# A spectral mixer with an MLP on one core: another element order in the array behind the first transform's last stage, and four placed pieces moved by one or two steps

## The chip, the cores and the metric

The kernel runs on one core of a Trainium2 chip. The metric is the device time of one execution in microseconds (us). Five engines work side by side, each through its own queue in order: PE (matrix multiplication; it first loads a stationary operand, the weights, and then streams the moving one), ACT and DVE (elementwise work, and copies out of PE's result memory PSUM into the working memory SBUF, called evictions here), POOL and SP (in this kernel almost only queues that start DMA transfers). An engine that waits for another holds up everything behind it in its own queue.

## The reference: what is computed

```
X = np.fft.rfft(x, axis=1)                      # x: 8 batches x 3008 rows x 256 channels
Y = X * (filt_r + 1j * filt_i)                  # one complex factor per frequency and channel
y = np.fft.irfft(Y, n=3008, axis=1)             # back to 24064 rows x 256
h = y @ w_in                                    # 256 -> 2048
g = np.maximum(h, 0.0) + alpha * np.minimum(h, 0.0)
out = g @ w_out                                 # 2048 -> 256
```

Inputs and output are fp32; the kernel works in fp16 with fp32 sums in PSUM.

## The kernel before, in words

3008 = 94 x 32, so each transform is two short ones with a factor between them. Both are matrix multiplications with constant tables. A batch goes through stages a (94-point, forward), b (32-point with factors, and the filter multiplied in on DVE), c (32-point back) and d (94-point back). Between a and b, and between c and d, rows and columns must change places.

**Batches one to seven** (class Fft) change them by writing to DRAM and reading back. Their pieces are placed among the steps of the MLP. The MLP runs over 48 blocks of 512 rows (the sixth of every twelve has 384); each block has 16 steps; a step is `up(j)` (two matmuls of w_in, L481; at odd j the eviction L490 on ACT, then L493 and L495 on DVE) and `down(j)` of the block before (matmuls of w_out, L512, with the eviction L517). `put(step, fn, ...)` writes a list by hand: a piece stands ahead of `up` in its step, and in the steps of the set `front` (those with a piece_a or a piece_c of batches one to seven) `down` stands ahead of both. Nothing reorders this later: the place in the program is the place in each engine's queue.

**Batch zero** (class First) has nothing to hide behind. It runs ahead of the blocks and changes rows and columns on PE, by a multiplication with the unit matrix `id16`:

- `piece_a` (L280) evicts into `am`, which lies in the array gtb, in runs of four results that stand 32 elements apart.
- `turn_at` (L290) turns `am` into `at`, evicted by ACT.
- The loop over kp = 0 to 11 (from L409) issues piece_b of kp + 2 (L299 on PE into one of two hps buffers, then the multiplication L304 on DVE that makes uu), then piece_c of kp (L324, 16 matmuls of 64 columns). Two kp share a pair of psO banks, `ops[0]` and `ops[1]`; the pool psO has just two, so piece_c of the next pair waits for the evictions of this one.
- After every odd kp up to 9, `keep_c` (L333) copies both banks on ACT into the array v (seen flat as `vm`), 512 results in each copy. kp 10 and 11 have copies of their own with 256 results; the second copy of kp 11 is on DVE. All these copies have the line of their helper: L255 on ACT, L258 on DVE.
- After kp 1, 3 and 5 comes a turn_at for later kp. After kp 7, 8 and 9, and within kp 11, stand two matmuls each (`warm`, L376) whose result nobody reads.
- After kp 5, a memset on DVE (L420) is followed on POOL's queue by the loads of w_in, w_out and batch one's x (L422, L424, L112). Behind them come the copies that make `filts_s`, wanted by batch one's piece_b and by the sign changes `neg` (L558) from step 26 on.
- `half_t` and `piece_t` then call `turn` (L340): for one of the 32 time positions s and one half f of the channels, 96 columns of v are the weights (L346) and `id16` streams. Four half_t come ahead of the blocks, the rest (piece_t) in steps 0, 3, 19, 23, 32 and 34.
- `half_d` and `pair_d` (L232) are stage d: eight matmuls for a pair_d into the one buffer of the pool psF, then an eviction into yT, the MLP's input. piece_b of batch one uses psF too (from step 36, every six steps), and DVE frees it at the end of L187.

In both versions a result of keep_c has four indices besides its partition (a channel): g (16: half f and group of four positions), e (4: position within the group), q (4) and k (24). A row of 96 weights is all (q, k) of one g and e. The array's order is e, g, q, k before, the last index running fastest.

Blocks of 512 rows read yT in order: group three of batch zero (rows 2256 to 3007) is first read in step 64, batch one's first group in step 96.

Of the kernel before, what the change touches and what calls it, by code (L numbers as in the profile page):

```python
# [15 lines left out]
NK = 24  # L16
# [34 lines left out]
def kernel(  # L51
# [211 lines left out]
    class First(Fft):  # L263
# [67 lines left out]
            on_act(o, w.unsqueeze(2).to_broadcast([128, 2 * (kb - ka), 2, 32]))  # L331

        def keep_c(self, kp, evicts, n=2):  # L333
            vm = self.vm.rearrange("p (e g q k) -> p g q k e", q=4, k=NK, e=4)
            for e in range(2):
                k = 2 * kp + e
                evicts[e](vm[:, :, :, k : k + 2 * n - 1 : 2],
                          self.ops[e][:, 0:n].rearrange("p k (g q e) -> p g q k e", q=4, e=4))

        def turn(self, pt, i, n):  # L340
            m = self.vm.rearrange("p (e g m) -> p g m e", m=96, e=4)
            for u in range(n):
                for f in range(2):
                    o = 256 * (u % 2) + 128 * f
                    s = n * i + u
                    nc.tensor.matmul(pt[0:96, u // 2, o : o + 128], m[:, 8 * f + s // 4, :, s % 4], id16,  # L346
                                     start=True, stop=True)
# [175 lines left out]
    def put(step, fn, *args):  # L523
        plan.setdefault(step, []).append((fn, args))

    def plan_fft(b, a_at, ta, quarters, x_at, b_at, add, c_at, d_at):
        f = Fft(b)
        for i in range(8):
            put(a_at[i], f.piece_a, i)
            front.add(a_at[i])  # L530
        for c in range(4):
            put(a_at[2 * c + 1], f.save_a, c)
            if b + 1 < NB:
                put(x_at[c],
                    lambda b=b, c=c: xc.update({(b + 1, c): load_x(b + 1, c)}))
        for q in range(quarters):
            w = NK // quarters
            put(ta, f.turn_a, nc.sync, w * q, w * q + w)
        for q in range(6):
            put(b_at[q], f.piece_b, q, not add)  # L540
            if add:
                put(b_at[q] + add, f.piece_s, q)
        for q in range(6):
            put(c_at[q], f.piece_c, q)
            front.add(c_at[q])
            if q % 2 == 1:
                put(c_at[q] + 1, f.turn_c, q // 2)
        for i in range(8):
            put(d_at[i], f.pair_d, i, on_act)

    for g, ts, ds, te, de in ((1, (0, 3), (6, 12), on_act, both[::-1]), (2, (19, 23), (25, 28), on_dve, (on_dve, on_dve)),
                              (3, (32, 34), (39, 45), on_act, (on_act, on_act))):
        for i in range(2):
            put(ts[i], f0.piece_t, 2 * g + i, te)
            put(ds[i], f0.pair_d, 2 * g + i, de[i])
# [7 lines left out]
    def d_steps(p):  # L563
        return [p + t for t in (91, 93, 104, 108, 116, 120, 140, 152)]

    plan_fft(1, range(12, 28, 2), 28, 4, (34, 42, 54, 66), range(36, 72, 6), 0, range(48, 84, 6),
             (91, 93, 97, 100, 111, 121, 142, 154))
    plan_fft(2, (50, 56, 62, 68, 74, 80, 82, 84), 90, 4, (57, 69, 81, 89),
             (106, 116, 126, 136, 148, 158), 7, (116, 126, 136, 148, 158, 172), d_steps(96))
    for b in range(3, NB):  # L570
        p = 96 * (b - 1)
# [54 lines left out]
```

## Time and profile before

| | |
|---|---|
| three runs | 813.82, 807.13, 810.01 us; median 810.01 |
| the profiled execution | 808.31 us; the span of its trace 806.5 us |
| busy in the span | PE 773.3 us (96%), ACT 606.3 (75%), DVE 596.8 (74%), POOL 142.2 (18%) |
| mean granted clock of PE | 0.977 |
| DMA | 100.64 MB, mean 125 GB/s |

How to read the lines below: in a timeline, start and length come first, then the engine, the line of the kernel, the operation, and output <- input with the shape; "x2" merges neighbours; what stands in brackets is the engine's idle time ahead of the instruction and what ended it. Grouped lines end with total busy time, mean of one in ns, and idle time by what ended it. In the slices of the page each digit is a fortieth of the span (about 20 us), in tenths. A tile's view lists minimum, median and maximum in ns, and who waited for it how long in all and how often.

### The profile page before, as it was taken

Reading aid. Unit: us, or ns where it says so; the run is one execution under the profiler, and the core shown is the slowest. Engines: PE = TensorE matmul, PEld = TensorE weight load, DVE = VectorE, ACT = ScalarE, POOL = GpSimd, SP = SyncE. Lnnn points to the kernel's source line nnn. Section 1 sums busy time; section 2 is a strip of 40 time slices with the busy share of each in tenths; the row PEclk is TensorE's granted clock in tenths of the full one; section 3 lists DMA queues with packets and bytes.
Section 4 is the critical chain, followed back from the end, with each engine's and each line's share of the span. In section 5 each row is a group of like instructions: output and inputs, shape, how many; then the busy total and the mean of one; then the engine's idle time right before and its main releaser. Section 6 shows DMA issues by size and latency. Waiting matters only on the chain.

```text
span 806.5 us, 16086 instructions
## 1 busy us (share of the span) xinstructions
PE 773.3 (96%) x6349; PEld 512.2 (64%) x6349; DVE 596.8 (74%) x1116; ACT 606.3 (75%) x673; POOL 142.2 (18%) x271
## 2 busy tenths in 40 slices
PE   7558999999999999999999999999999999999997
PEld 4334656666666666766666666666666666776665
DVE  4427888578887788687886788778886888766664
ACT  4868778788876887688876887688877777676764
POOL 6320056113200122012200221001110111000000
PEclk9559999999999999999999999999999999999999
DMA  9596469875674555935675464843366232521111
GB/s 184 84 174 149 131 97 208 191 200 139 169 145 131 109 140 125 216 91 129 152 136 139 96 165 106 177 127 97 104 130 161 66 87 72 131 66 33 41 40 52
DMA packets 95083, 100.64 MB, mean 125 GB/s; under 512 B 11280, under 2 KB 82464, under 8 KB 94816
## 3 DMA queue, kind: packets, MB, share of 16 engines
q1 hardware_dynamic: 80368, 70.25, 33.4%
q0 software_dynamic: 14640, 29.38, 21.1%
q8 instruction: 49, 0.80, 0.4%
q14 instruction: 26, 0.21, 0.1%
HBM read 55.28 MB, written 46.66 MB: 126 GB/s over the span
## 4 chain that ended last, share of the span: by engine, by line
PE 88%; ACT 6%; DMA 2%; DVE 2%; issue 1%; POOL 0%; ACTq 0%; DVEq 0%; POOLq 0%
PE hps L481 39%; PE op L512 39%; ACT v L255 3%; PE hps L155 3%; PE psF L232 3%; PE psF L179 2%; ACT gtb L490 1%; PE hps L210 1%; DMA uu<-ww 1%; DMA xs<-in_x_dram 1%; PE op L324 1%; DMA zt<-v_dram 1%; DVE ww L186 1%; DVE uu L187 1%; DVE m L493 1%
## 5 line engine op out<-in xcount | busy, mean ns | idle before, releaser
L490 ACT ACTIVATE gtb<-hps 128x1024 f16<-128x1024 f32 (+1 forms) x384 | 385.6, 1005 | 130.4 <-PE hps L481 129.5
L512 PE MATMUL op<-wout_s,gtb 128*128 128x256 f16 x3008 | 435.8, 273 | 0.1
L481 PE MATMUL hps<-yT,win_s 128*128 128x512 f16 (+1 forms) x1536 | 434.0, 375 | 1.6 <-ACT gtb L490 1.4
L512 PEld LDWEIGHTS <-gtb 128*128 128x128 f16 x3008 | 293.9, 98 | 168.4 <-issue 0.4
L493 DVE TENSOR_SCALAR m<-gtb,alm_s 128x512 f16<-128x512 f16 (+1 forms) x768 | 232.9, 346 | 151.2 <-ACT gtb L490 150.4
L495 DVE TENSOR_TENSOR gtb<-gtb,m 128x2048 f16<-128x2048 f16 (+1 forms) x192 | 231.0, 1203 | 10.4 <-PE hps L481 0.5
L481 PEld LDWEIGHTS <-win_s 128*128 128x128 f16 x1536 | 142.5, 98 | 61.2 <-issue 14.7
L193 POOL DMA_DIRECT2D sw<-ww x144 | 70.9, 500 | 381.6 <-DVE ww L186 378.6
L255 ACT ACTIVATE asb<-hps 96x1024 f16<-96x1024 f32 x56 | 57.1, 1020 | 12.0 <-PE hps L155 11.5
L517 ACT ACTIVATE osb<-op 128x512 f32<-128x512 f32 (+1 forms) x97 | 56.2, 580 | 5.3 <-issue 2.8
L255 ACT ACTIVATE yT<-psF 128x752 f16<-128x752 f32 x59 | 47.1, 798 | 12.8 <-PE psF L232 12.7
L112 POOL DMA_DIRECT2D xs<-in_x_dram x64 | 39.2, 709 | 91.1 <-PE hps L155 79.4
L255 ACT ACTIVATE v<-hps 128x1024 f16<-128x1024 f32 x42 | 43.0, 1024 | 15.4 <-PE hps L210 15.4
L186 DVE TENSOR_TENSOR ww<-psF,filts_s 128x1024 f16<-128x1024 f32 x42 | 51.1, 1217 | 0.0
L187 DVE TENSOR_TENSOR uu<-psF,filt_s 128x1024 f16<-128x1024 f32 x42 | 51.0, 1213 | 0.0
L232 PE MATMUL psF<-wi_s,zt 96*128 96x94 f16 x500 | 31.3, 206 | 3.3 <-DVE uu L187 2.6
L155 PE MATMUL hps<-xs,wf_s 94*96 94x512 f16 x112 | 33.5, 380 | 0.6 <-ACT asb L255 0.6
L232 PEld LDWEIGHTS <-zt 96*128 96x128 f16 x512 | 28.7, 99 | 6.8 <-DVE uu L187 3.2
L255 ACT ACTIVATE v<-op 128x512 f16<-128x512 f32 (+1 forms) x12 | 25.5, 2376 | 6.2 <-PE op L324 6.2
L191 POOL DMA_DIRECT2D uu<-ww x24 | 19.3, 1229 | 40.8 <-DVE uu L187 35.6
L304 DVE TENSOR_TENSOR uu<-hps,filt_s 128x1024 f16<-128x1024 f32 x11 | 13.4, 1222 | 17.0 <-PE hps L299 14.6
L198 DVE TENSOR_TENSOR uu<-uu,sw 128x1024 f16<-128x1024 f16 x36 | 24.6, 684 | 0.1
(67 smaller groups left out, 197.6 us busy)
## 6 DMA issues: line engine op xcount, KB each, us to landing
out_dram<-osb SPq DMA_DIRECT2D x160, 128.0 KB
a_dram<-asb SPq DMA_DIRECT2D x28, 384.0 KB
v_dram<-v SPq DMA_DIRECT2D x84, 128.0 KB
zt<-v_dram SPq DMA_DIRECT2D x28, 384.0 KB
sw<-ww POOLq DMA_DIRECT2D x144, 64.0 KB, 2.4
at<-a_dram SPq DMA_DIRECT2D x20, 384.0 KB
xs<-in_x_dram POOLq DMA_DIRECT2D x32, 192.0 KB, 4.3
xs<-in_x_dram POOLq DMA_DIRECT2D x32, 184.0 KB, 6.0
```

Of the source, the lines that this page charges most:

```text
L155: nc.tensor.matmul(ps[0:96, u], wf1_s, xs[:, o : o + 512], start=True, stop=True)
L186: nc.vector.tensor_mul(ww, px, fs)
L187: nc.vector.tensor_mul(uu, px, f)
L193: nc.gpsimd.dma_start(out=sw[o : o + 32], in_=ww[i : i + 32])
L232: nc.tensor.matmul(ps[:, m], self.zt[:, 8 * g + 4 * mh + m, dh * 128 : dh * 128 + 128], wi3_s, start=True, stop=True)
L255: nc.scalar.activation(o, i, AF.Copy)
L481: nc.tensor.matmul(self.hps[:, j % 2, 0:tn], win_s[:, kt, j * 128 : (j + 1) * 128], yT[:, kt, self.t0 : self.t0 + tn], start=(kt == 0), st ...
L490: nc.scalar.activation(g[:, 2 * i : 2 * i + 2], self.hps[:, :, 0:tn], AF.Copy)
L493: nc.vector.tensor_scalar(m[:, 2 * i + h], g[:, 2 * i + h], 0.0, a, OP.min, OP.mult)
L495: nc.vector.tensor_add(g, g, m)
L512: nc.tensor.matmul(self.op[:, si - s0], self.gts[k][:, 128 * si : 128 * si + 128], wout_s[:, k], start=(si == s0 and k == 0), stop=(si == ...
L517: nc.scalar.activation(osb[:, 0:m], self.op[:, 0:m], AF.Copy)
```

## The change

```diff
         def keep_c(self, kp, evicts, n=2):
-            vm = self.vm.rearrange("p (e g q k) -> p g q k e", q=4, k=NK, e=4)
+            vm = self.vm.rearrange("p (g q k e) -> p g q k e", q=4, k=NK, e=4)
...
         def turn(self, pt, i, n):
-            m = self.vm.rearrange("p (e g m) -> p g m e", m=96, e=4)
+            m = self.vm.rearrange("p (g m e) -> p g m e", m=96, e=4)
...
-                              (3, (32, 34), (39, 45), on_act, (on_act, on_act))):
+                              (3, (32, 34), (41, 47), on_act, (on_act, on_act))):
...
     plan_fft(1, range(12, 28, 2), 28, 4, (34, 42, 54, 66), range(36, 72, 6), 0, range(48, 84, 6),
-             (91, 93, 97, 100, 111, 121, 142, 154))
+             (92, 94, 97, 100, 111, 121, 142, 154))
```

The order in v becomes g, q, k, e: the four e of one (g, q, k) stand side by side (8 bytes of fp16), and the 96 weights of one g and e stand 4 elements apart instead of side by side. Copies and loads have the same number, shape and place in the queues. Two pair_d of batch zero's group three stand two steps later, and batch one's first two one step later; on PE and ACT they pass the matmuls and the evictions of those steps. The queues of DVE, POOL and SP hold the same instructions in the same order.

## The prediction

> **What bounds the kernel now.** I read the slices of the page first, then its chain and its groups. PE is at 9 tenths or more in nearly every slice after 60 us, so that part is worth only what PE itself saves. The slices from 20 to 60 us stand apart: PE at 5, ACT at 7 or 8, the granted clock at 5.
>
> ```profile
> PE   7558999999999999999999999999999999999997
> ACT  4868778788876887688876887688877777676764
> PEclk9559999999999999999999999999999999999999
> PE 88%; ACT 6%; DMA 2%; DVE 2%; issue 1%; POOL 0%; ACTq 0%; DVEq 0%; POOLq 0%
> L255 ACT ACTIVATE v<-op 128x512 f16<-128x512 f32 (+1 forms) x12 | 25.5, 2376 | 6.2 <-PE op L324 6.2
> ```
>
> Half of ACT's 6% of the chain is line 255 writing v: the evictions of the first transform's last stage, 2.4 us for 512 elements. The view of tile v tells who waits for them:
>
> ```profile
> L346 PEld LDWEIGHTS <-v x64: 119/123/203, 57.2 to 94.7; 128*96 128x96 f16 x64
> L255 ACT ACTIVATE v<-op x12: 1316/2407/2712, 20.4 to 53.0; 128x512 f16<-128x512 f32 x10, 128x256 f16<-128x256 f32 x2
>   PE op L324: 16.0, 10
> ```
>
> The timeline of one pair of kp shows the loop that this makes (start, length, then what it waited for):
>
> ```profile
> 26.71 1.04 PE L290 MATMUL psF<-id,gtb 128*128 128x128 f16 x8
> 26.80 4.62 ACT L255 ACTIVATE v<-op 128x512 f16<-128x512 f32 x2 [0.93 <-PE op L324]
> 30.93 1.34 ACT L255 ACTIVATE at<-psF 128x1024 f16<-128x1024 f32 x1
> 31.48 0.21 PE L324 MATMUL op<-twi_s,uu 64*128 64x64 f16 x1 [2.01 <-ACT v L255]
> 31.98 0.64 PE L299 MATMUL hps<-at,gtb 64*64 64x256 f16 x8
> 32.68 1.22 DVE L304 TENSOR_TENSOR uu<-hps,filt_s 128x1024 f16<-128x1024 f32 x1 [3.08 <-PE hps L299]
> 33.20 4.63 ACT L255 ACTIVATE v<-op 128x512 f16<-128x512 f32 x2 [0.93 <-PE op L324]
> ```
>
> A round takes 33.20 - 26.80 = 6.4 us: two evictions (4.62), then the next pair of piece_c, held until both psO banks are empty. DVE waits 3 us a round for the same reason. The eviction is the bound here.
>
> **Part 1: the evictions.** Before, keep_c puts four neighbouring results 1536 elements apart, so every 2-byte result goes to a place of its own; after, four stand side by side (8 bytes), in a row of 96 per (q, k). What such a write costs is in the trace: piece_a's eviction also writes runs of four, 32 elements apart, and reads PSUM with a jump at every element. Its row stands beside dense ones (form by form):
>
> ```profile
> L255 ACT ACTIVATE gtb<-hps 128x768 f16<-128x768 f32 x3 | 2.4, 810 | 6.6 <-PE hps L280 6.6
> L255 ACT ACTIVATE zt<-op 96x512 f16<-96x512 f32 x1 | 0.6, 592 | 2.1 <-PE op L346 2.1
> L255 ACT ACTIVATE zt<-psF 96x1024 f16<-96x1024 f32 x4 | 4.1, 1024 | 0.9 <-PE psF L346 0.9
> ```
>
> Dense costs 592 ns at 512 and 1024 at 1024: 0.84 ns an element and some 160 fixed. At 768 that gives 808, and the scattered reader with runs of four took 810. So runs of four are free, and so is the jumping read; I take 592 ns for 512 (from 2310, half of 4.62) and an estimated 380 for 256. The other end is today's 2310. The Trainium skill (Advanced Engine Details and Errata, SBUF Cachelines) says two or more accesses to a 16-byte line run at full rate and a new line per access is penalised; the trace agrees, 2310 against 592, and by it the sum would be the same.
>
> Now the loop's new length, from where ACT ends its table copy (20.5 us, unchanged) to the first half_t:
>
> ```profile
> 20.42 4.61 ACT L255 ACTIVATE v<-op 128x512 f16<-128x512 f32 x2
> 23.75 1.22 DVE L304 TENSOR_TENSOR uu<-hps,filt_s 128x1024 f16<-128x1024 f32 x1 [2.47 <-DMA filt_s<-in_filt_r_dram]
> 33.85 0.06 DVE L420 MEMSET win_s<- 128x1 uint32 x1
> 34.22 1.09 POOL L422 DMA_DIRECT2D win_s<-in_moe_w_in_dram  x2 [9.59 <-DVE win_s L420]
> 37.06 2.12 POOL L112 DMA_DIRECT2D xs<-in_x_dram  x4
> 55.87 1.30 DVE L258 CAST v<-psF 128x256 f16<-128x256 f32 x1 [8.19 <-ACT v L255]
> 56.69 1.95 POOL L434 DMA_DIRECT2D filts_s<-filt_s  x4 [6.58 <-DMA filt_s<-fst]
> 57.23 1.09 PE L346 MATMUL op<-id,v 128*96 128x128 f16 x8 [1.69 <-DVE v L258]
> 61.91 1.46 PE L481 MATMUL hps<-yT,win_s 128*128 128x512 f16 x6
> 69.53 0.60 PE L155 MATMUL hps<-xs,wf_s 94*96 94x512 f16 x2
> ```
>
> The fifth multiplication (kp 4) waits for its filter until 23.75 whatever ACT does. Eight multiplications follow, 8 x 1.22 = 9.8, so uu of kp 11 can't exist before 33.5, and with the last piece_c and its eviction half_t can't start before about 34.5. That is the floor. Walking the loop: a round is the two evictions (1.18), piece_c, piece_b, piece_c on PE (about 0.55 each at the half clock of these rows: piece_c's rest runs from 31.48 to 31.98, piece_b's 0.64 has its tail in it) and waits of some 0.2, about 3.05 us; two warm matmuls (an estimated 1.0: they stream the 1024 columns that L290's eight do in 1.04) come after each of kp 7, 8 and 9. From 23.75 this gives keep of kp 2/3 at 23.0, 4/5 at 27.4, 6/7 at 30.7, 8/9 at 34.8, kp 11 done at 38.7. With PE's terms halved (full clock) DVE's 2 x 1.22 and ACT's 1.18 and 1.34 (the eviction of at) a round set 2.5 us, and kp 11 is done at 35.8. I take 37.0, between them: 57.23 - 37.0 = **20.2 us less**, ends 17.7 (with another us of waits) and 22.7 (the floor).
>
> What else hangs on this: L420's memset stands behind the multiplication of kp 7, at 28.6 instead of 33.85. So win_s, wout_s, batch one's x and fst's copy on POOL's queue come 5.2 us sooner, not 20. Their cover:
>
> ```profile
> win_s<-in_moe_w_in_dram POOLq DMA_DIRECT2D x2, 512.0 KB, 6.4
> xs<-in_x_dram POOLq DMA_DIRECT2D x4, 192.0 KB, 12.3
> 87.61 0.61 DVE L558 TENSOR_SCALAR filts_s<-filts_s,sgn_s 128x1536 f16<-128x1536 f16 x1
> ```
>
> win_s, issued at 29.0 and landing 6.4 us later, is there at 35.5 to 36; the first block, 4.7 us behind half_t, starts at 41.3. Batch one's first x (37.06 + 12.3 - 5.2 = 44.2) is wanted at 69.53 - 20.6 = 48.9. filts_s, copied from 51.5 instead of 56.69, is wanted by the sign change at 87.6 - 20.6 = 67. All covered, by 5, 5 and a few us; if a cover went, that much of the gain would go. With that DMA traffic nearer to the first blocks I add nothing.
>
> **Part 2: the weight loads.** turn now loads its 96 columns with a step of 4 elements (8 bytes). No load in the trace has a step. Today eight pairs take 0.45 us (94.34 to 94.79; the third row is the next step's first matmul, so a step is 0.87):
>
> ```profile
> 94.34 0.61 PE L346 MATMUL psF<-id,v 128*96 128x128 f16 x8
> 94.79 0.59 PE L481 MATMUL hps<-yT,win_s 128*128 128x512 f16 x2
> 95.66 0.59 PE L481 MATMUL hps<-yT,win_s 128*128 128x512 f16 x2
> ```
>
> That is 56 ns each, 128 columns streaming, with the load hidden below. The row nearest to a stepped access is the old eviction, (2310 - 160) / (592 - 160) = 5 times a dense element; five times at most 56 ns is 280, 0.22 more for each of 64 loads: **+14 us at most**. A gain is excluded, since the load is hidden today. I take 0: the moving operand of L324 also hops between runs, and the trace has no PE read slowed by its pattern. Half of that factor (2.5) would cost 0.084 x 64 = 5.4. The Trainium skill speaks against zero: Vector Engine (DVE) Microarchitecture Reference, Measured stream behaviour on trn2, says a VectorE port keeps its rate only for runs of two adjacent 4-byte words and takes up to 2.5 times when stepping single words; by it, if it holds for PE's port, the sum would be about 5 us higher; no run here shows it yet.
>
> **Part 3: the clock in between.** Stretches of 1 us (last columns: granted clock, DMA share, GB/s; PE's busy time comes first):
>
> ```profile
> 21.00:22.00 1.00, 0.24 (x8) 0.09 (x1) 0.29 (x1) 1.00 (x1) 0.53 (x1) 1.00 1.36 194
> 22.00:23.00 1.00, 0.14 (x1) 0.10 (x1) 0.00 (x0) 1.00 (x2) 0.48 (x1) 0.82 0.98 127
> 60.00:61.00 1.00, 0.95 (x13) 0.65 (x11) 0.69 (x2) 0.74 (x2) 0.00 (x0) 0.90 1.06 184
> ```
>
> The clock fell soon after PE went idle at 21.2 and came back at 60.1, after 3 us of turns. In the new loop PE is busy nearly throughout, so it should come back in the 30s. The turns after the loop, 16 pairs at half clock, would save 16 x 0.05 = 0.8; I count **0.4**.
>
> **Part 4: the moved steps.** Rows of the stalls:
>
> ```profile
> 101.54 0.51 PE L232 MATMUL psF<-wi_s,zt 96*128 96x94 f16 x8 [1.80 <-DVE uu L187]
> 108.56 0.51 PE L232 MATMUL psF<-wi_s,zt 96*128 96x94 f16 x8 [0.84 <-DVE uu L187]
> 156.89 0.51 PE L232 MATMUL psF<-wi_s,zt 96*128 96x94 f16 x8 [0.52 <-DMA zt<-v_dram]
> ```
>
> Group three's pair_d (eight matmuls and one ACT eviction each, no DMA) waits at steps 39 and 45 until VectorE frees the only psF buffer. Two steps are 2 x 0.87 = 1.74 us, so at 41 and 47 the waits are about 0.06 and 0. Late next: piece_b at 42 and 48 wants psF back one step later, while ACT's eviction (an estimated 0.79 for 752 by the slope above, and 0.23 of waits) has 0.87 of cover, so 0.15 each. Gain 2.64 - 0.06 - 0.3 = **2.3**, ends 1.0 (ACT late with its queue) and 2.6. yT of group three is wanted at step 64, far off. On ACT each eviction now stands behind one gtb eviction more; POOL's and SP's queues are unchanged. Batch one's first pair_d goes from 91 to 92: one step of 384 columns (an estimated 0.76) covers the 0.52, gain **0.5**. The next from 93 to 94: its yT is wanted at step 96, 1.5 us of steps against 1.05; nothing, or up to -0.5 if ACT is late.
>
> **Sum.** 20.2 + 0 + 0.4 + 2.3 + 0.5 = 23.4. The profiled execution took 808.3 us (span 806.5), 1.7 under the median of the three runs; 808.3 - 23.4 = 784.9, and on the median's basis **786.6 us**.
>
> **Rivals.**
> 1. The clock stays at full rate. The Trainium skill (TensorE: Matmul & The Clock Gate, Part 1) lets it fall only after an idle window of about 3.4 us; the trace speaks against that, 0.82 within 2 us of the last long run. But if the shorter gaps do hold it, the loop ends at 35.8 and the turns save 0.8: 21.4 + 0.8 + 2.8 = 25.0, 785.0 us.
> 2. The stepped load costs 2.5 times: 18.0 in all, 792.0 us. For it: the old eviction's price for hopping. Against it: two elements still share 16 bytes.
> 3. Data arrives late: win_s or x only 5.2 us sooner. If landing took 5 us longer than its cover, 791.6. Against it: by L422's row POOL had issued nothing for 9.59 us ahead of win_s, so nothing stands before it.
> 4. The eviction doesn't get cheaper, its cost being in the read of two banks' halves (k jumps 1 KB). Then only the steps count: 807.2 us. Against it: piece_a's row, a jump per element at no cost.
> 5. Slower than before: the load is so slow with a step that it eats the gain. It must cost 23.4 / 64 = 0.37 us more each to tie, 0.49 to be 1% slower (then 818). L346's loads take 0.12 to 0.20 today with their latency, and the bound above is 0.22, so this needs a price outside the trace.
>
> **How the numbers follow.** Forecast 0.50, rival one 0.28, two 0.10, three 0.05, four 0.04, five 0.03. Low end: the floor (22.7) with 0.8, 2.6 and 0.5 is 26.6, so 783.4, less half of the runs' scatter below the median (2.9): 782. High end: 17.7 + 0 + 1.0 + 0 with rival two's 5.4 leaves 13.3: 796.7, say 797. That holds some 0.85. One per cent of 810, 8 us, is about what a measurement of this kernel can tell from no change. Faster by more: 0.50 + 0.28 + 0.10 + 0.05 = 0.93; within: 0.04; slower: 0.03.
>
> **What would show it.** v's evictions at about 0.6 us and 512 elements, two in 1.2; DVE's waits in the loop near zero; half_t at 36 to 38; the first L481 at about 41; L346's eight pairs still at 0.45; L232's waits on uu gone. It would be wrong if the evictions stayed over 1 us, if L346's pairs spread, or if L481 or L155 began to wait for a DMA.

## The result, and the profile after

The changed kernel takes 789.38 us (median of six runs, 787.85 to 790.63); the kernel before 810.19 us beside it. The ratio is 0.9733, 95% interval 0.9699 to 0.9767. The forecast was 786.6 (782 to 797). The profiled execution took 787.85 us (span 786.0), 20.5 less than the one before.

First the page's slices of the changed kernel, then its tile v, then one row of the groups by form, before and after.

```profile
PE   7889999999999999999999999999999999999997
ACT  4578787887778887798777887788876777677663
PEclk9899999999999999999999999999999999999999
```

```profile
L346 PEld LDWEIGHTS <-v x64: 163/186/188, 37.1 to 77.1; 128*96 128x96 f16 x64
L255 ACT ACTIVATE v<-op x12: 378/594/606, 20.5 to 35.6; 128x512 f16<-128x512 f32 x10, 128x256 f16<-128x256 f32 x2
  PE op L324: 1.0, 3
```

```profile
L255 ACT ACTIVATE v<-op 128x512 f16<-128x512 f32 x10 | 23.1, 2554 | 5.5 <-PE op L324 5.5
L255 ACT ACTIVATE v<-op 128x512 f16<-128x512 f32 x10 | 5.4, 596 | 6.2 <-PE op L324 6.2
```

The hole between 20 and 60 us is gone. An eviction of 512 results into v went from 2554 to 596 ns (2310 to 540 where two follow each other and the pair's time is halved), and PE's wait for it from 16.0 to 1.0 us. The loads, however, went from a median of 123 to 186 ns. Where the time went is read best by landmarks, the same instruction in both timelines. Rows of the changed kernel:

```profile
20.48 1.08 ACT L255 ACTIVATE v<-op 128x512 f16<-128x512 f32 x2
23.63 4.62 DVE L304 TENSOR_TENSOR uu<-hps,filt_s 128x1024 f16<-128x1024 f32 x4 [2.44 <-DMA filt_s<-in_filt_r_dram]
28.20 0.06 DVE L420 MEMSET win_s<- 128x1 uint32 x1
37.14 0.93 PE L346 MATMUL op<-id,v 128*96 128x128 f16 x8
40.64 0.84 PE L346 MATMUL psF<-id,v 128*96 128x128 f16 x8 [0.38 <-DVE yT L258]
41.32 1.46 PE L481 MATMUL hps<-yT,win_s 128*128 128x512 f16 x6
49.09 0.60 PE L155 MATMUL hps<-xs,wf_s 94*96 94x512 f16 x2
55.62 1.01 PE L155 MATMUL hps<-xs,wf_s 94*96 94x512 f16 x2
79.10 0.41 PE L179 MATMUL psF<-at,twf_s 64*64 64x256 f16 x8
92.07 0.39 PE L210 MATMUL hps<-uu,twi_s 64*64 64x256 f16 x8
```

And those of the kernel before that the prediction does not show:

```profile
61.46 0.61 PE L346 MATMUL psF<-id,v 128*96 128x128 f16 x8 [0.36 <-DVE yT L258]
73.99 0.60 PE L155 MATMUL hps<-xs,wf_s 94*96 94x512 f16 x2
96.62 0.41 PE L179 MATMUL psF<-at,twf_s 64*64 64x256 f16 x8
112.28 0.39 PE L210 MATMUL hps<-uu,twi_s 64*64 64x256 f16 x8
```

| landmark | before | after | shift | change since the row above |
|---|---|---|---|---|
| first half_t | 57.23 | 37.14 | -20.1 | -20.1 |
| turn in step 0 | 61.46 | 40.64 | -20.8 | -0.7 |
| first piece_a of batch one (step 12) | 69.53 | 49.09 | -20.4 | +0.4 |
| third piece_a (step 16) | 73.99 | 55.62 | -18.4 | **+2.1** |
| first piece_b (step 36) | 96.62 | 79.10 | -17.5 | **+0.9** |
| first piece_c (step 48) | 112.28 | 92.07 | -20.2 | -2.7 |
| end of the span | 806.5 | 786.0 | -20.5 | -0.3 |

Three rows go the wrong way. The +0.4 and the +0.9 fit the stepped loads (two and four groups of eight pairs, 0.23 each: 0.46 and 0.92). The +2.1 stands in no term of the forecast. The chain of waits of the changed kernel names it, and the stretches of 1 us show what came with it (PE's busy time first, the granted clock third from the end):

```profile
44.02 6.36 DMA filt_s<-fst
51.12 1.02 ACT asb L255
```

```profile
51.00:52.00 1.00, 0.00 (x0) 0.00 (x0) 0.97 (x4) 0.88 (x1) 0.74 (x2) 1.00 0.00 0
54.00:55.00 1.00, 1.00 (x5) 0.37 (x4) 0.00 (x0) 0.00 (x0) 0.00 (x0) 0.50 0.64 148
```

`fst`, the first filter block in fp32, has the tag of `asb` (L269 and L145): both lie in one place. Batch one's first eviction into asb must wait until the copy of fst to filt_s has read it. That copy stands in POOL's queue behind the memset, the weights and batch one's x, so it came only 5.5 us sooner (44.02 instead of 49.54) while the steps came 20 us sooner. ACT waited for it, then PE, and the clock fell behind the gap.

### The profile page after: what moved, and what is told of

Same layout as the page of the kernel before. It is cut to its first block, busy times and chain, and to the rows that moved or that the text cites. A ratio compares the mean times of both kernels' runs of the same rounds, so it can differ in the third digit from the quotient of the medians.

```text
span 786.0 us, 16085 instructions
## 1 busy us (share of the span) xinstructions
PE 769.7 (98%) x6349; PEld 511.8 (65%) x6349; DVE 595.5 (76%) x1116; ACT 587.0 (75%) x673; POOL 142.7 (18%) x271
## 4 chain that ended last, share of the span: by engine, by line
PE 92%; DMA 4%; issue 1%; POOL 1%; ACT 1%; DVE 1%; POOLq 0%; ACTq 0%; DVEq 0%
PE op L512 41%; PE hps L481 41%; PE hps L155 3%; PE psF L232 3%; DMA filt_s<-in_filt_r_dram 2%; PE psF L179 2%; PE hps L210 1%; DMA uu<-ww 1%; DMA filt_s<-fst 1%; POOL xs L112 1%; PE psF L346 0%; PE op L324 0%; ACT gtb L490 0%; PE hps L299 0%; PE psF L376 0%
## 5 line engine op out<-in xcount | busy, mean ns | idle before, releaser
L481 PE MATMUL hps<-yT,win_s 128*128 128x512 f16 (+1 forms) x1536 | 434.8, 375 | 1.2 <-ACT gtb L490 1.1
L481 PEld LDWEIGHTS <-win_s 128*128 128x128 f16 x1536 | 142.8, 98 | 61.5 <-issue 15.4
L186 DVE TENSOR_TENSOR ww<-psF,filts_s 128x1024 f16<-128x1024 f32 x42 | 51.1, 1218 | 0.0
L155 PE MATMUL hps<-xs,wf_s 94*96 94x512 f16 x112 | 33.9, 384 | 1.4 <-ACT asb L255 1.4
L232 PEld LDWEIGHTS <-zt 96*128 96x128 f16 x512 | 28.6, 98 | 2.9 <-issue 0.6
L210 PE MATMUL hps<-uu,twi_s 64*64 64x256 f16 x336 | 16.8, 271 | 1.1 <-DMA uu<-ww 1.1
L179 PE MATMUL psF<-at,twf_s 64*64 64x256 f16 x336 | 17.3, 281 | 0.0
```

The source lines that it names most:

```text
L155: nc.tensor.matmul(ps[0:96, u], wf1_s, xs[:, o : o + 512], start=True, stop=True)
L186: nc.vector.tensor_mul(ww, px, fs)
L232: nc.tensor.matmul(ps[:, m], self.zt[:, 8 * g + 4 * mh + m, dh * 128 : dh * 128 + 128], wi3_s, start=True, stop=True)
L481: nc.tensor.matmul(self.hps[:, j % 2, 0:tn], win_s[:, kt, j * 128 : (j + 1) * 128], yT[:, kt, self.t0 : self.t0 + tn], start=(kt == 0), st ...
```

## The experiments

**The order alone, and the steps alone.** The first kernel has the new order and the old steps, the second the reverse.

```diff
# e1_layout_only, against the changed kernel
-(3, (32, 34), (41, 47), ...   (92, 94, 97, 100, ...
+(3, (32, 34), (39, 45), ...   (91, 93, 97, 100, ...
# e2_moves_only, against the kernel before
-(3, (32, 34), (39, 45), ...   (91, 93, 97, 100, ...
+(3, (32, 34), (41, 47), ...   (92, 94, 97, 100, ...
```

> The new order in v alone, all four steps back in their old places. Mine: the steps gave what their stalls were worth (between step 32 and the third pair_d of batch one the changed kernel gains another 2.7 us and 0.6 us on the kernel before), so this one is 2.8 us slower than the changed kernel's 789.4: about 792.2, and line 232 waits again for VectorE at steps 39 and 45, 2.6 us in all. Rival: the steps' gain is given back further on by a DMA wait, and this one lies at 789.5 to 790.5 with shorter waits later.

> The steps alone, the old order in v. Mine: the stalls at steps 39 and 45 (1.80 and 0.84) and the one at step 91 (0.52) go, some 0.3 comes at the next piece_b: 810.2 - 2.7 = 807.5. Rival, given back: 809.5 to 810.2. In this kernel line 255 still needs 2.3 us for 512 results, so it also shows that the steps have no part in the gain ahead of the blocks.

Measured: the order alone 0.9752 of the kernel before (0.9719 to 0.9785), the steps alone 0.9945 (0.9921 to 0.9968), which is 4.5 us with an interval from 2.6 to 6.4. The forecast for the steps, 2.7, lies at the edge of that interval, and the order alone can't be told from the changed kernel by its total. PE's waits in the kernel with the order alone:

```profile
PE psF L232 <- DMA zt<-v_dram: 3.3, 1, 3.3
PE psF L232 <- DVE uu L187: 2.6, 2, 1.8
```

The 2.6 us of steps 39 and 45 are back, and they are absent in the kernel with the steps alone: by the traces the forecast of 2.7 for that part holds, and the totals of the two parts add up within their intervals. The wait of 3.3 us for zt at step 91 is new; more of it below.

**The copy of fst issued first.**

```diff
+            nc.gpsimd.dma_start(out=filt_s[:, 0:1], in_=f0.fst)
             nc.vector.memset(win_s[:, 0, 0:2], 0.0)
...
-    nc.gpsimd.dma_start(out=filt_s[:, 0:1], in_=f0.fst)
```

> The changed kernel, with the copy of fst to filt_s issued ahead of the weights on POOL's queue instead of behind batch one's x. Mine: asb and fst share one place in SBUF, so the first eviction into asb waits until that copy has read fst; in the changed kernel this lands at 51.0 us, the eviction is late by 1.2 us and PE's clock falls to 0.50 behind the gap (53 to 56 us). Without it the 2.1 us lost between the first and the third piece_a come back: 789.4 - 2.1 = 787.3, the eviction follows its matmul by 1 us and the clock stays at 1.00 there. Rival: the eviction waits for the matmul or for an older eviction, as its row says (0.74 until line 481), and nothing moves: 789.4.

Measured: 0.9688 (0.9657 to 0.9720), 787.44 us on a chip where the kernel before took 813.3. The interval overlaps that of the changed kernel, so the trace has to decide. The eviction follows its matmul directly, and the wait ahead of the second piece_a is what it was before the change:

```profile
49.70 0.60 PE L155 MATMUL hps<-xs,wf_s 94*96 94x512 f16 x2
50.88 1.02 ACT L255 ACTIVATE asb<-hps 96x1024 f16<-96x1024 f32 x1
51.95 0.59 PE L155 MATMUL hps<-xs,wf_s 94*96 94x512 f16 x2 [0.57 <-ACT asb L255]
```

From half_t to the last turn this kernel needs 37.9 us (37.8 to 75.7), the changed one 40.0 (37.1 to 77.1): the 2.1 us. The rival, that the wait was line 481's as its row says, falls. The totals agree: the three kernels with the early copy and this order of v (two of them, with seven matmuls more, come below) have ratios of 0.9680 to 0.9688, the changed kernel, its repeat and the two more with the late copy 0.9721 to 0.9733.

**The loads without a step.**

```diff
-            m = self.vm.rearrange("p (g m e) -> p g m e", m=96, e=4)
+            m = self.vm.rearrange("p (e g m) -> p g m e", m=96, e=4)
```

> The changed kernel, but turn reads 96 columns that stand side by side, as before; the positions are mixed up by that, all else is the same. Mine: the step costs (0.68 - 0.45) / 8 = 29 ns a load, 64 loads, 1.8 us: 789.4 - 1.8 = 787.6, the loads' median back from 186 to about 123 ns. Rival: the pairs are hidden behind the evictions of zt, and this gives 0.5 us or less: 789.0.

```profile
L346 PEld LDWEIGHTS <-v x64: 119/123/123, 36.0 to 76.0; 128*96 128x96 f16 x64
```

```profile
PE hps L155 <- ACT asb L255: 3.0, 1, 3.0
PE psF L232 <- DMA zt<-v_dram: 2.2, 1, 2.2
```

Measured: 0.9721 (0.9688 to 0.9755), no better than the changed kernel. The loads are dense again and eight pairs take 0.45 us, yet the total did not follow: the first piece_a came sooner and waited 3.0 instead of 1.4 us for the copy of fst. My number (1.8 us in the total) was wrong for this kernel, and so was the rival's reason; the price is real where it is paid, but what is saved ahead of step 12 (32 of the 64 loads) runs into the same wait. The other 32 loads, some 0.9 us, are less than these intervals can show, and in this profile the wait of 2.2 us for zt hides them.

**The changed kernel again, and with two additions.** The second kernel has the early copy and seven matmuls without use, where PE idles ahead of the fifth multiplication.

```diff
             if kp < 7:
                 f0.turn_at(kp + 5, 2, on_act)
+            if kp == 3:
+                warm(7, bank("o"))
```

> The changed kernel once more, as the reference for the kernels beside it on the same chip. Its ratio to the kernel before was 0.973; the same is expected, with line 155's wait for asb (1.4 us and the half clock behind it) in the profile again. If that wait is not there, its cause is another than the copy of fst.

> The changed kernel with the copy of fst ahead of the weights, and with seven more matmuls nobody reads (1.5 us at full clock) behind the second turn_at, where PE is idle from 23.3 to 24.9 us. Mine: PE's clock falls at about 26 because of that gap; with it filled the clock stays at 1.00, the first half_t stands 1 us earlier (36 instead of 37.1 to 37.8) and the total is 3 us under the changed kernel on this chip. Rival one: the fall has another cause (it came 3 us behind the gap), the clock falls all the same, and only the 2 us of fst are won. Rival two: DVE's multiplications, 1.22 us each from 23.7 on, set the loop's end at either clock: clock at 1.00, but half_t no earlier.

Measured: 0.9721 (0.9690 to 0.9752) for the changed kernel, 0.9680 (0.9646 to 0.9715) with both additions. The repeat tells most. In its profile the clock did not fall in the loop:

```profile
26.00:27.00 1.00, 0.75 (x25) 0.50 (x25) 1.00 (x2) 0.00 (x0) 0.00 (x0) 1.00 0.03 4
35.42 0.93 PE L346 MATMUL op<-id,v 128*96 128x128 f16 x8
51.75 1.02 ACT L255 ACTIVATE asb<-hps 96x1024 f16<-96x1024 f32 x1 [3.09 <-DVE gtb L495]
```

half_t came 1.7 us sooner than in the first profile, the eviction into asb 0.6 us later, and the total was the same. PE waited 3.8 us for that eviction, where it had waited 1.4, and the clock fell during this wait (at 51.7 us). The row blames a DVE instruction for the 3.09 us; in other runs it blames line 481 or nobody.

**The seven matmuls alone.**

> The changed kernel with only the seven matmuls nobody reads behind the second turn_at, the copy of fst in its old place. Mine: PE's clock stays at 1.00 in the loop and half_t stands 1 to 2 us earlier, but the first eviction into asb comes at 50.8 to 51.8 us whatever the loop does, because the copy of fst lands then; so the total is that of the changed kernel, ratio 0.972 to 0.973 (789 us), and PE's wait before the second piece_a is longer than 1.4. Rival: the total falls with the loop, by 1.5 us or more (ratio 0.970 or less), and the wait for asb is not what set the end.

Measured: 0.9724 (0.9699 to 0.9749), the changed kernel's ratio, as the first of the two accounts had it.

```profile
35.66 0.93 PE L346 MATMUL op<-id,v 128*96 128x128 f16 x8
51.31 1.02 ACT L255 ACTIVATE asb<-hps 96x1024 f16<-96x1024 f32 x1 [2.40 <-issue]
```

Four profiles with half_t at 35.4, 35.7, 36.0 and 37.1 us (the repeat, this kernel, the one with dense loads, the first) have this eviction at 51.8, 51.3, 50.8 and 51.1. The copy sets it, and POOL's next instruction, which by its own row waits for this copy, shows it (the changed kernel, its repeat, the dense loads):

```profile
51.26 1.96 POOL L434 DMA_DIRECT2D filts_s<-filt_s  x4 [6.66 <-DMA filt_s<-fst]
51.88 1.95 POOL L434 DMA_DIRECT2D filts_s<-filt_s  x4 [6.75 <-DMA filt_s<-fst]
50.95 1.95 POOL L434 DMA_DIRECT2D filts_s<-filt_s  x4 [6.06 <-DMA filt_s<-fst]
```

In all seven profiles with this order or another in v and the copy in its old place, ACT's first eviction into asb starts 0.13 or 0.14 us ahead of that instruction, whomever the row blames. (In the kernel with both additions the clock was at 0.50 from 20.6 to 24 us, ahead of the seven matmuls, and at 1.00 from then on. Its half_t, at 36.7, came no earlier than the repeat's, 35.4, and its ratio is that of the early copy alone, 0.9688, within the intervals: a gain by the seven matmuls is not shown.)

**Other steps of the weight load.** The six piece_t read with steps 1, 2, 3, 8, 16 and 32.

```diff
-            m = self.vm.rearrange("p (g m e) -> p g m e", m=96, e=4)
+            t = 4 if n == 2 else (1, 2, 3, 8, 16, 32)[i - 2]
...
-                    nc.tensor.matmul(..., m[:, 8 * f + s // 4, :, s % 4], id16,
+                    nc.tensor.matmul(..., self.vm[:, s : s + 95 * t + 1 : t], id16,
```

> The changed kernel, but the weights of turn are read with other steps: 4 elements in the four half_t as now, and then 1, 2, 3, 8, 16 and 32 in the six piece_t (steps 0, 3, 19, 23, 32, 34); what is read is not the right element, the counts are. Eight pairs now take 0.45 us at step 1 and 0.68 at step 4. Theory A (pairs of words, by the page on VectorE's streams): step 2 is as dense, 3 and more all cost the same 0.68. Theory B (16-byte lines): 0.45 up to a step of 4 is refuted by the 0.68 already unless the rate goes by the bytes touched; then 2 is between, 8 and more cost twice what 4 does, up to 0.9 or 1.4 us for eight.

It was executed once (790.32 us). Its timeline, from the start of each group of eight to the next L481 (steps 2, 3, 8 and 16):

```profile
42.07 0.61 PE L346 MATMUL psF<-id,v 128*96 128x128 f16 x8
42.52 1.47 PE L481 MATMUL hps<-yT,win_s 128*128 128x512 f16 x6
...
59.45 0.69 PE L346 MATMUL psF<-id,v 128*96 128x128 f16 x8
59.97 0.59 PE L481 MATMUL hps<-yT,win_s 128*128 128x512 f16 x2
...
64.32 1.45 PE L346 MATMUL psF<-id,v 128*96 128x128 f16 x8
65.61 0.59 PE L481 MATMUL hps<-yT,win_s 128*128 128x512 f16 x2
...
74.97 1.54 PE L346 MATMUL psF<-id,v 128*96 128x128 f16 x8
76.35 0.59 PE L481 MATMUL hps<-yT,win_s 128*128 128x512 f16 x2
```

0.45, 0.52, 1.29 and 1.38 us; step 1 gave 0.45 (40.33 to 40.78), step 32 1.26 (78.09 to 79.35), step 4 gives 0.68 in the changed kernel. Theory A falls, since step 8 costs twice what step 4 does. (It carried over to PE's loads what the Trainium skill, Vector Engine (DVE) Microarchitecture Reference, Measured stream behaviour on trn2, says of VectorE's ports.) Theory B holds in the form that the time goes by the 16-byte lines that the 96 columns touch: 36 lines at step 3 take 65 ns a pair, 48 at step 4 85, 96 at step 8 161, and wider steps, with 96 lines as well, cost about the same (172 and 158). Below an estimated 30 lines (56 ns at some 1.8 a line) the streaming of 128 columns (56 ns) hides the load.

**Other runs of the eviction.**

```diff
+            va = self.vm[:, 0:3072].rearrange("p (y k e) -> p y k e", k=12, e=2)
+            vb = self.vm[:, 3072:6144].rearrange("p (x c e u) -> p x c e u", c=6, e=4, u=2)
...
+                if kp < 6:    # into va[:, :, k : k + 2 * n - 1 : 2]
+                else:         # into vb[:, :, kp - 6 : kp - 6 + n, :, e]
...
```

> The changed kernel with two other orders of v's elements: for kp 0 to 5 runs of two results (4 bytes) that stand apart, for kp 6 to 11 single results 4 bytes apart, four of them within 16 bytes; turn reads side by side, so positions are mixed up. Theory A (what counts is 4 or 8 adjacent bytes for a write): the runs of two cost more than 592 ns for 512 results and the singles cost nearly the old 2300. Theory B (16-byte lines, two or more accesses to a line are enough): the singles cost 592, since four fall into a line, and the runs of two as well. Theory C (every jump costs, whatever its length): runs of two cost half of the old price, about 1250, singles 2300.

```profile
27.03 1.08 ACT L255 ACTIVATE v<-op 128x512 f16<-128x512 f32 x2 [0.61 <-PE op L324]
29.30 1.36 ACT L255 ACTIVATE v<-op 128x512 f16<-128x512 f32 x2 [0.26 <-PE op L324]
```

It was executed once (787.58 us). Two banks in runs of two take 1.08 us, as with runs of four; single results 4 bytes apart take 1.36. Theories A and C fall (the singles are far from the old 4.6), theory B holds but for a quarter on top of the singles. One thing stayed the same in all these orders: counted from the start of v, the four neighbouring results of one instruction fall into one 16-byte line (with runs of two, the pairs of k and k + 2 stand 8 bytes apart). What a pair alone on its line costs was not tried.

**The order of pairs.** Step 2 and runs of two are both free, so an order with both should beat the order of four. It is written with two instructions for each bank.

```diff
+            vm = self.vm.rearrange("p (h x k e) -> p h x k e", h=2, k=NK, e=2)
...
+                o = self.ops[e][:, 0:n].rearrange("p k (x h e) -> p h x k e", h=2, e=2)
+                for h in range(2):
+                    evicts[e](vm[:, h, :, k : k + 2 * n - 1 : 2], o[:, h])
...
+            m = self.vm.rearrange("p (h g m e) -> p h g m e", h=2, m=96, e=2)
+                    nc.tensor.matmul(..., m[:, s % 4 // 2, 8 * f + s // 4, :, s % 2], id16,
```

> The kernel with the early copy of fst and the seven matmuls, and v in a third order: pairs of results side by side, the two pairs of a group in different halves of v, so that a weight row has a step of 2 elements; each bank is evicted in two instructions of 256 results. Mine: eight pairs of turn take 0.45 us again, as step 2 did, which is 64 x 0.029 = 1.8 us less; the evictions cost 2 x 0.38 instead of 0.59 a bank, some 0.3 us on the way since DVE sets the loop's pace; in all 1.5 us under the kernel beside it with the order of four (ratio 0.966 against 0.968). Rival: ACT becomes the bound of the loop (two banks 1.5 and at 1.03 a round, more than DVE's 2.44), half_t comes 1 us later and nothing is won.

> The kernel with the early copy of fst and the seven matmuls once more, as the reference for the order of pairs beside it. Its ratio to the kernel before was 0.968, and the same is expected here; the first eviction into asb at about 50 us follows its matmul by 1.2 us.

Measured: 784.41 us, 0.9669 (0.9640 to 0.9697), the lowest ratio here; beside it the order of four 785.68 us, 0.9686 (0.9657 to 0.9715). The size is as expected, but the intervals overlap, so the totals don't show that the order of pairs is faster by 1.5 us. The traces show its parts: step 0's eight pairs take 0.61 in the row where they took 0.84, and the four instructions of two banks 1.21 where two took 1.08. half_t came at 35.95 against 34.92, the 1 us of the rival, but not for its reason: the fifth multiplication, which waits for its filter, already started at 24.00 against 23.27, and from there to half_t the order of pairs takes 0.3 more, as forecast. From half_t to batch one's first piece_b it takes 38.3 where the order of four takes 39.9.

## Why the prediction was right

The forecast of the time held, and so did its largest term. Of the signs that were to show it wrong two came all the same: L346's eight pairs spread from 0.45 to 0.68, and L155 began to wait for a DMA, by way of asb. They cost 1.9 and 2.1 us, a tenth each of what the evictions gave.

**The loop (part 1) was right**: half_t at 37.14 against 37.0. That it was right to 0.1 us is luck: 37.0 was taken between two ends, and the same kernel's repeat had half_t at 35.42. The price from piece_a's row held (596 ns against 592; 378 for 256 against 380), and so did what came next: the fifth multiplication at 23.63, the memset at 28.20 against 28.6. The walk's ends were 38.7 at half clock and 35.8 at full clock. Seen were 37.14 and, with the early copy, 37.76 with the clock down for 6.8 us of the loop, and 35.42 with the clock up.

**The loads (part 2) were not free.** I took 0, with 5.4 as the rival and 14 as the bound. They cost 29 ns each, 64 x 0.029 = 1.9 us. The failing step is "the trace has no PE read slowed by its pattern": true, but no row had a load with a step, so it excluded nothing. The Trainium skill (SBUF — State Buffer, Door 1: The DMA port swizzle, in its note on cachelines) lets a stride of up to 8 bf16 elements, which are as wide as fp16, pass free; the trace disagrees for this load, 85 ns at a step of 4 and 161 at 8 against 56 dense. The Trainium skill (Vector Engine (DVE) Microarchitecture Reference, Measured stream behaviour on trn2), which part 2 set against zero, gives 2.50 ns a column for stepped single words against 1.05. That is a factor of 2.4 and not the 2.5 that I wrote; the estimate of 5 us stays. It was right that the step costs something, but its rule doesn't have the doubling from step 4 to step 8.

**The clock in between (part 3)** was sized too low: the turn stage gained 0.7 against 0.4, and that with 0.5 of stepped loads (16 x 0.029) already taken off, so 1.2 without them. Rival one's time, 785.0 us, did not come even where its condition did, for the reason that follows.

**The covers failed in one place.** I wrote that "fst's copy" moves by 5.2 us, and asked whether filts_s, the copy behind it, comes in time. It did. I did not ask who waits for the place that fst leaves; asb does, through a shared tag. That is close to rival three, something on POOL's queue 5 us sooner and the steps 20, at 2.1 us instead of 5; but rival three looked for data that come late, and this is a place that comes free late. It also caps part 1: a loop that ends sooner only waits longer.

**The moved steps (part 4)**: 2.7 between steps 36 and 48 against 2.3 forecast. The 0.5 at step 92 is open. Of the twelve profiles with all or a part of the change, seven show no wait for zt there and five one of 1.6 to 3.3 us, four of these with the step at 92. zt's landing varies by more than one step of cover, so this gain is there in some executions only; what makes it vary was not tried.

In sum: 23.4 forecast, 20.5 measured between the two profiles. The loads took 1.9 and fst's copy 2.1, the later moved steps gave 0.2 less and the loop 0.1 less; the turn stage gave 0.8 more than forecast and the first moved steps 0.4 more. That leaves 20.3; the rest is rounding. The two large misses point one way, and the smaller ones took back a part of them.

## What to carry to other kernels

When an array is written by one engine and read as weights by another, count the 16-byte lines on both sides: here two pairs of two-byte results on a line were enough for the writer, and a step of two elements was the last one free for the load. When a stage becomes shorter, list everything that its old length covered, and for each buffer in reach who inherits its place: two tiles with one tag are a wait that no instruction of the code names. When an engine's wait is put down to an instruction that had long ended, look among the transfers, and compare kernels: a time that stays put while all around it moves belongs to what sets it.

## What the runs showed of the hardware

- A load of 96 weight columns takes about 1.7 to 1.8 ns for each 16-byte line it touches at full clock: 65, 85 and 161 ns a pair at 36, 48 and 96 lines.
- ACT writes 512 two-byte results in some 0.59 us in runs of four or of two, four results to a line in both; in 0.76 as singles, four to a line; in 2.55 as singles that each go to another line than the one before.
- The granted clock fell to 0.50 in or behind PE gaps of 1.2 to 3.8 us, fourteen times between 20 and 55 us in the profiles with a new order in v, but not behind the gap of 1.5 us in the repeat of the changed kernel, though one of 1.25 was enough in the kernel with both additions. So the length of the gap alone doesn't decide. It came back 3.4 to 3.5 us after the fall eleven times and 6.8 to 6.9 three times. The Trainium skill (TensorE: Matmul & The Clock Gate, Part 1) tells of a free-running window of about 3.4 us and of one kernel that behaves differently from run to run by its phase. That fits these executions, though most of the gaps were shorter than the idle window of 3.4 us that it names.
